# A planned order for linear attention and a two-layer network: first loads, normalisation statistics, one tile's transposition and the planner's model of the DMA queues

## The chip, the cores and the metric

The kernel runs on one core of a Trainium2 chip. The metric is the device time of one execution in microseconds; the median of the runs is used. Three runs of the kernel before gave 218.5, 219.17 and 219.6 us, so the median is 219.17 us.

A core has five engines with a queue of instructions each: PE (matmuls and transposes), DVE and ACT (work on vectors), POOL (work on vectors, and the issuing of DMAs that convert the type on the way) and SP (here only the issuing of DMAs). They run side by side and wait for each other through semaphores. DMA transfers run beside them.

## The reference

Inputs are q, k and v of shape (4 batches, 8 heads, 768 steps, 64), a gain vector of 512 and two weight matrices, 512 x 2048 and 2048 x 512, all fp32. First a recurrence over the steps, with a decay of its own for each head:

```python
gamma = 1.0 - 2.0 ** (-5.0 - np.arange(H, dtype=np.float32))
for t in range(S):
    state = gamma[None, :, None, None] * state + np.einsum('bhd,bhe->bhde', k[:, :, t], v[:, :, t])
    y[:, :, t] = scale * np.einsum('bhd,bhde->bhe', q[:, :, t], state)
```

with scale 1/8. Its result, laid out as (4, 768, 512), is x. Then each row of x is normalised and goes through the two layers:

```python
mu = np.mean(x, axis=-1, keepdims=True)
var = np.mean((x - mu) ** 2, axis=-1, keepdims=True)
xn = (x - mu) / np.sqrt(var + 1e-06) * g_ln
ch = np.maximum(xn @ w_ch1, 0.0) @ w_ch2
return (x + ch).astype(np.float32)
```

## The kernel before

**Tiles.** The 4 x 768 rows are cut into 24 tiles of 128 rows. Tiles 0 to 3 are the first 128 steps of the four batches; then come the five others of batch 0 (tiles 4 to 8), of batch 1 (9 to 13), and so on.

**Attention, per tile.** q and k have to be transposed. For tiles below `T0 = 8` PE does it (lines 395 and 402): ACT copies the transposed k to "trk" (L184) and DVE scales the transposed q into "trq" (L407). From tile 8 on q and k are loaded as a pair into one "qk" buffer, and a DMA on SP's queue transposes the pair into "tr" (L417); DVE then scales the q half into "trq" (L424). PE multiplies the two to the scores "pa" (L434), DVE multiplies them by the decay mask into "asb" (L441), and PE forms y, "py", from asb and v (L457), and from trq and the running state where there is one (L453). For the state, POOL scales v by the decay into "vg" (L510), PE multiplies it with k, "pd" (L522), and DVE turns that into the state in bf16 (L536).

**Normalisation, per tile.** For tiles from 4 on DVE takes the mean and the variance from py with `bn_stats` and `bn_aggr` (L491, L492), then forms xn = (y − mean) · gain (L466), and ACT copies y to "x_all" (L497). For tiles 0 to 3 ACT copies y with a sum on the side (L473), DVE scales the sum to the mean (L479), and ACT squares with another sum, into a "junk" tile, and scales it to the variance (L484, L486). The factor 1/sqrt(var) is applied at the very end: ACT takes the root per group (L572), DVE the reciprocal (L578).

**Layers, per group.** Tiles are grouped for the first layer: six groups of one tile, three of two, three of four. xn is transposed, by PE for tiles below `TX = 8` (L550, copied by ACT to "xnt") and by a DMA on SP's queue from tile 8 on (L564). The first layer (L597) is cut into blocks of 16, 8 or 4 matmuls, which fill one "mm" buffer (there are two); ACT or DVE applies the relu into "h" (L610, L612). The second layer (L634) has four blocks of four matmuls per tile; DVE multiplies by 1/sqrt(var) and adds x (L642), and SP stores the result (L649).

**Loads.** q, k and v tiles (128 KB each in bf16) and the eight weight blocks (512 KB each in bf16) are loaded by POOL's DMAs, which convert from fp32 (L338, L346). Only tile 0 is loaded as fp32 (L324): k and v over SP's queue, q over ACT's, and then cast by ACT and DVE.

**The order.** The order of all instructions is computed before the kernel is built. Every piece of work is a task with an engine (or several to choose from), an estimated duration, a rank, the tasks that it needs, and the buffers that it takes and uses. `Plan.order` simulates the engines with these estimates: it always takes the task that can start first, and among equals the one with the lower rank. What it writes down is the order of the instructions on each engine; times and buffers in the simulation are estimates, and the waits in the built program follow from the data and from the buffers that the tile pools really hand out. In the simulation a task that takes a buffer waits for the buffer of its pool that has been held longest (`oldest = held[name][0]`, lines 68 to 74). Loads share one DMA queue of the model: each occupies it for its estimated time (`dma_free`), and a load may be issued at most `ahead` = 6000 ns before the queue is free. Transpositions by DMA get a fixed latency (`load` 1500, `lat` 5000 for qk; 800 and 4500 for xn), loads from tile 8 on 1500 ns more, and vg from tile 8 on 2500 ns more, so that what uses them is planned later. The first loads of POOL have a fixed rank, in the list `first` (lines 351 to 354). `Plan.fill` puts matmuls on zeros into PE's gaps of the first 20 us (L658).

Of the kernel before, what the change touches and what calls it, by code (L numbers as in the profile page):

```python
# [9 lines left out]
FP32 = mybir.dt.float32  # L10
BF16 = mybir.dt.bfloat16
AF = mybir.ActivationFunctionType
ALU = mybir.AluOpType

PE, ACT, DVE, POOL, SP = range(5)


class Plan:
# [6 lines left out]

    def __init__(self, seen, begin, load_lat, ahead):
        self.seen, self.begin, self.load_lat, self.ahead = seen, begin, load_lat, ahead  # L30
        self.tasks, self.bufs = [], {}
# [4 lines left out]
    def add(self, eng, ns, rank, emit, after=(), takes=None, uses=(), load=0, lat=0, at=0,  # L36
            follows=()):

        t = {"on": eng if isinstance(eng, dict) else {eng: ns}, "rank": rank, "emit": emit,
             "after": list(after), "takes": takes, "uses": list(uses) + ([takes] if takes else []),
             "load": load, "lat": lat, "at": at, "follows": list(follows)}
        self.tasks.append(t)
        return t

    def order(self):
# [8 lines left out]
        dma_free, out = 0, []  # L57
        while any(todo.values()):
            best = None
            for e in engines:  # L60
                for t in todo[e]:
                    if any("end" not in d for d in t["after"] + t["follows"]):
                        continue
                    at = max(free[e], t["at"], dma_free - self.ahead if t["load"] else 0)
                    for d in t["after"]:
                        at = max(at, d["end"] if d["eng"] == e and not d["load"] else d["seen"])
                    at = max([at] + [d["end"] for d in t["follows"]])
                    if t["takes"]:
                        name = t["takes"][0]
                        if len(held[name]) == self.bufs[name]:  # L70
                            oldest = held[name][0]
                            if left[oldest]:
                                continue
                            at = max(at, ends[oldest])
                    if best is None or (at, t["rank"]) < best[0]:
                        best = (at, t["rank"]), t, e
# [8 lines left out]
            if t["load"]:  # L85
                dma_free = max(dma_free, t["end"]) + t["load"]
                t["seen"] = dma_free + self.load_lat + t["lat"]
# [25 lines left out]
def kernel(  # L113
# [21 lines left out]
    P = 128  # L135
# [7 lines left out]
    GROUPS = [1] * 6 + [2] * 3 + [4] * 3  # L143
# [3 lines left out]
    T0, TX = 8, 8  # L147
# [9 lines left out]
                {PE: 900, ACT: 800, DVE: 900, POOL: 1300, SP: 800}, 2250, 6000)  # L157
    ps = bass.MemoryType.PSUM

    def make_pool(name, n, space=None):  # L160
# [7 lines left out]
        for name, n, space in (  # L168
            ("k0", B, None), ("v0", B, None), ("qsb", 6, None), ("ksb", 5, None), ("vsb", 5, None),
            ("qk", 4, None), ("tr", 4, None), ("vg", 3, None), ("trq", 3, None), ("trk", 3, None),  # L170
# [40 lines left out]
    junk = const.tile([P, DM], BF16, name="junk")  # L211
# [77 lines left out]
    def c_gb(eng):  # L289
# [4 lines left out]
        out=grow, in_=moe_g_ln.rearrange("(o n) -> o n", o=1)), load=10)  # L294
# [13 lines left out]
    def load(kind, j, rank):  # L308
        takes, uses, follows = None, [], []
        if kind in "qkv":  # L310
            b, c = TILES[j]
            src = {"q": q, "k": k, "v": v}[kind][b].rearrange("h (c p) d -> c p h d", p=P)[c]
            ns, dma = 910, 780
# [6 lines left out]
            if j == 0:  # L320

                def emit32(eng):
                    dst = take("osb", kind, [P, DM], FP32).rearrange("p (h d) -> p h d", d=D)
                    (nc.scalar if eng == ACT else nc.sync).dma_start(out=dst, in_=src)  # L324
                raw = a(ACT if kind == "q" else SP, 390, -200 + "kqv".index(kind), emit32, (),
                        ("osb", kind), (), 900)

                def emit(eng):
                    evacuate(eng, take(*takes, [P, H, D], BF16),
                             held["osb", kind].rearrange("p (h d) -> p h d", d=D))  # L330
                loaded[kind, j] = a({"k": {ACT: 620}, "q": {DVE: 490}, "v": {ACT: 620, DVE: 430}}[kind], 0, -60, emit,
                                    [raw], takes, [("osb", kind)])
# [6 lines left out]
        else:  # L339
# [3 lines left out]
            ns, dma = 820, 2900  # L343

            def emit(eng):
                nc.gpsimd.dma_start(out=dst, in_=src)  # L346
        loaded[kind, j] = a(POOL, ns, rank, emit, (), takes, uses, dma, 1500 if kind in "qkv" and j > 7 else 0,
                            follows=follows)


    first = ["iota", "pos", "k1", "q1", "v1", "w1_0", "k2", "q2", "v2", "w1_1", "k3", "q3", "v3",
             "w1_2", "k4", "q4", "v4", "w1_3", "k5", "q5", "v5"]
    pool_rank = {x: i - 1000 for i, x in enumerate(first)}
# [7 lines left out]

# [15 lines left out]
    for t in range(NT):  # L377
        g, i = group_of[t]
        rank_of[t] = 10 * t if t < 4 else max(10 * t, 500 + unit["1", g, 0] - 48 + 8 * i)
# [4 lines left out]
    for t in range(NT):  # L384
# [4 lines left out]
        xi = x0 + i4  # L389

# [24 lines left out]
        else:  # L415
            def e_tr(eng, t=t):
# [4 lines left out]
                   1500, 5000)  # L421
# [16 lines left out]
        pat = a(PE, 340, r + 1.2, e_pa, [eq, ek], ("pa", t), [("trq", t), kt])  # L438
# [8 lines left out]
        def e_py(eng, t=t, c=c):  # L447
# [8 lines left out]
            for h in range(H):  # L456
# [6 lines left out]
                ("py", t), [("asb", t), ("trq", t), where["v", t]] + ([("pb", t)] if c else []))  # L463
# [6 lines left out]
        if t < 4:  # L470

            def e_xc(eng, t=t):
                nc.scalar.activation(  # L473
                    out=x_all[:, t, :], in_=held["py", t].rearrange("p h d -> p (h d)"),
                    func=AF.Copy, accum_out=bns[:, t, 0:1])
            xc = a(ACT, 650, r + 2, e_xc, [pyt], uses=[("py", t)])

            def e_me(eng, t=t):
                nc.vector.tensor_scalar_mul(out=mv[:, t, 0:1], in0=bns[:, t, 0:1], scalar1=1.0 / DM)  # L479
            me = a(DVE, 100, r + 2, e_me, [xc])  # L480
            xnn = a(DVE, 750, r + 2, e_xn, [me, gl], ("xn", t), [("py", t)])

            def e_va(eng, t=t):
                nc.scalar.activation(out=junk, in_=x_all[:, t, :], func=AF.Square,  # L484
                                     bias=mv[:, t, 0:1], scale=-1.0, accum_out=bns[:, t, 1:2])
                nc.scalar.activation(out=mv[:, t, 1:2], in_=bns[:, t, 1:2], func=AF.Copy,  # L486
                                     scale=1.0 / DM)
            bn = a(ACT, 900, r + 100, e_va, [me, xc], at=28000 + 2000 * t)
        else:
            def e_bn(eng, t=t):  # L490
                nc.vector.bn_stats(out=bns[:, t, :], in_=held["py", t].rearrange("p h d -> p (h d)"))  # L491
                nc.vector.bn_aggr(out=mv[:, t, :], in_=bns[:, t, :])  # L492
            bn = a(DVE, 880, r + 2, e_bn, [pyt], uses=[("py", t)])
            xnn = a(DVE, 750, r + 3, e_xn, [bn, gl], ("xn", t), [("py", t)])

            def e_xc(eng, t=t):
                nc.scalar.copy(out=x_all[:, t, :].rearrange("p (h d) -> p h d", d=D),  # L497
                               in_=held["py", t])
            xc = a(ACT, 590, r + 2, e_xc, [xnn], uses=[("py", t)])


        if c > 0:
            for cc in ([0, 1] if c == 1 else [c]):
# [4 lines left out]
                def e_vg(eng, j=j, cc=cc):  # L508
# [6 lines left out]
                        lat=2500 if j > 7 else 0)  # L515
# [44 lines left out]
        else:  # L560
            def e_ex(eng, t=t, xb=xb, xi=xi):
                if xi == 0:
# [3 lines left out]
                      [("xn", t)] + ([("xnt", xb)] if xi else []), 800, 4500,  # L566
# [54 lines left out]
    for t, cols in [(t, slice(0, DM)) for t in range(NT - 1)] + [  # L621
# [29 lines left out]
        a(ACT if cols.start else SP, 350, 100, e_st, [add], uses=[("osb", key)])  # L651
# [42 lines left out]
```

## Time and profile before

| What | Value |
|---|---|
| Time, median of 3 runs | 219.17 us (218.5 to 219.6) |
| Span of the profiled execution | 221.8 us |
| PE busy | 209.4 us, 94% of the span |
| DVE, ACT, POOL busy | 118.8, 85.6, 89.3 us |
| First-layer matmuls (L597) | 93.9 us |
| Second-layer matmuls (L634) | 90.4 us |
| Transposition of a qk pair, issue to landing | 6.5 us, median of 16 |
| Transposition of an xn tile, issue to landing | 4.0 us, median of 16 |
| Load of 128 KB by POOL, issue to landing | 6.5 to 8.8 us, medians by kind |
| Load of a weight block, issue to landing | 9.5 us, median of 8 |

The profile is of one execution; the page gives its span and no other time for it. Names such as "tr<-qk" say what an instruction writes and what it reads, "L417" is a line of the kernel. A line of the waits reads: engine, what it was about to do and at which line, what it waited for, the time in total, how often, and the longest. A line of the chain in order of time has the start and the length in us, then what ran. In the slices each digit is a tenth of busy time in a fortieth of the span (5.5 us). "Issue to landing" is the time from a DMA's issue until its semaphore shows it done.

### The profile page before, as it was taken

The numbers are of one execution on the slowest core, as the hardware profiler recorded it, in microseconds if no ns is written. First come the engines' busy times: TensorE is split into PE (matmuls) and PEld (weight loads), VectorE is DVE, ScalarE is ACT, GpSimd is POOL, SyncE is SP. The second block draws the span as 40 slices with busy tenths as digits, with TensorE's granted clock in tenths as the row PEclk, the third lists the DMA queues.
The fourth block names the chain that finished last, engine by engine and source line by source line (L and its number), as shares of the span: only waits on it lengthen the run. The fifth ranks groups of instructions, "written<-read, shape, count | busy, mean of one in ns | idle before, by whom it ended". The sixth has DMA issues, their size and how long they took to land.

```text
span 221.8 us, 4587 instructions
## 1 busy us (share of the span) xinstructions
PE 209.4 (94%) x1896; PEld 131.4 (59%) x1896; DVE 118.8 (54%) x229; ACT 85.6 (39%) x166; POOL 89.3 (40%) x105
## 2 busy tenths in 40 slices
PE   6988999998999999979999958999999999999993
PEld 6677999975756557756676423544444444444453
DVE  6566697974248999959888526562521001111121
ACT  5455688653312113524326241464433343232000
POOL 8996898967065399809059450000000000000000
PEclk9699999999999999999999996999999999999999
DMA  7999999999999999999999999411120011100212
GB/s 145 177 179 181 177 156 204 203 154 109 177 149 158 202 148 136 181 129 187 164 207 110 163 170 126 114 24 24 50 71 14 33 47 50 47 21 26 95 50 95
DMA packets 108326, 26.91 MB, mean 121 GB/s; under 512 B 101009, under 2 KB 105361, under 8 KB 108306
## 3 DMA queue, kind: packets, MB, share of 16 engines
q0 software_dynamic: 75984, 13.24, 82.6%
q1 hardware_dynamic: 31138, 12.98, 31.0%
q10 hardware_dynamic: 1184, 0.39, 0.7%
q8 instruction: 15, 0.25, 0.5%
q14 instruction: 5, 0.04, 0.1%
HBM read 27.27 MB, written 6.29 MB: 151 GB/s over the span
## 4 chain that ended last, share of the span: by engine, by line
PE 75%; DMA 15%; DVE 6%; POOL 1%; issue 1%; POOLq 0%
PE tp L634 34%; PE mm L597 32%; DMA w<-in_moe_w_ch_dram 8%; DMA tr<-qk 7%; PE pa L434 2%; PE py L457 2%; DVE asb L441 2%; PE pd L522 2%; PE py L453 1%; DVE trq L424 1%; DVE osb L642 1%; DVE state L536 1%; DVE bns L491 1%; PE tp L402 0%; PE tp L395 0%
## 5 line engine op out<-in xcount | busy, mean ns | idle before, releaser
L597 PE MATMUL mm<-xnt,w 128*128 128x128 bf16 (+2 forms) x768 | 93.9, 273 | 0.2 <-DMA w<-in_moe_w_ch_dram 0.2
L634 PE MATMUL tp<-w,h 128*128 128x512 bf16 (+1 forms) x400 | 90.4, 375 | 0.6 <-DVE osb L642 0.6
L610 ACT ACTIVATE h<-mm 128x512 bf16<-128x512 f32 x87 | 51.9, 598 | 74.2 <-PE mm L597 74.0
L597 PEld LDWEIGHTS <-w 128*128 128x128 bf16 x768 | 58.3, 98 | 24.3 <-DMA w<-in_moe_w_ch_dram 0.3
L634 PEld LDWEIGHTS <-h 128*128 128x128 bf16 x400 | 38.6, 99 | 41.2 <-issue 2.8
L642 DVE SCALAR_TENSOR_TENSOR osb<-tp,rstd,x_all 128x512 f32<-128x512 f32 (+1 forms) x25 | 18.2, 727 | 63.4 <-PE tp L634 63.2
L441 DVE TENSOR_TENSOR asb<-pa,mask 128x1024 bf16<-128x1024 f32 x24 | 29.3, 1220 | 12.3 <-PE pa L434 12.3
L510 POOL TENSOR_TENSOR vg<-vsb,vsc 128x512 bf16<-128x512 bf16 x16 | 16.9, 1057 | 21.0 <-DMA vsb<-in_v_dram 21.0
L338 POOL DMA_DIRECT2D vsb<-in_v_dram x20 | 18.0, 903 | 4.2 <-PE py L457 2.9
L338 POOL DMA_DIRECT2D qk<-in_k_dram x16 | 14.5, 906 | 12.7 <-DMA tr<-qk 12.6
L497 ACT CAST x_all<-py 128x512 bf16<-128x512 f32 x20 | 11.7, 584 | 19.1 <-DVE xn L466 17.9
L466 DVE SCALAR_TENSOR_TENSOR xn<-py,mv,gb 128x512 bf16<-128x512 f32 x24 | 18.0, 751 | 0.9
L536 DVE TENSOR_TENSOR state<-pd,gch 64x256 bf16<-64x256 f32 x40 | 16.7, 418 | 1.8 <-PE pd L522 1.5
L491 DVE BATCH_NORM_STATS2 bns<-py 128x6 f32<-128x512 f32 x20 | 13.9, 694 | 5.4 <-PE py L457 5.1
L338 POOL DMA_DIRECT2D qk<-in_q_dram x16 | 14.4, 898 | 1.4 <-DMA w<-in_moe_w_ch_dram 1.4
L424 DVE TENSOR_TENSOR trq<-tr,qsc 128x512 bf16<-128x512 bf16 x16 | 7.8, 494 | 9.1 <-DMA tr<-qk 8.9
L457 PE MATMUL py<-vsb,asb 128*128 128x64 bf16 x160 | 8.1, 194 | 3.0 <-DVE asb L441 3.0
L457 PEld LDWEIGHTS <-asb 128*128 128x128 bf16 x192 | 8.1, 100 | 3.2 <-DVE asb L441 3.2
L658 PE MATMUL mm<-zeros 128*128 128x128 bf16 x86 | 8.3, 262 | 1.0 <-DVE zeros L218 1.0
L572 ACT ACTIVATE rstd<-mv,epsb 128x1 f32<-128x1 f32 (+2 forms) x12 | 3.2, 294 | 13.7 <-DVE mv L492 13.7
L453 PEld LDWEIGHTS <-trq 128*128 128x128 bf16 x80 | 6.0, 98 | 3.2
L434 PE MATMUL pa<-trq,tr 64*128 64x128 bf16 x128 | 6.4, 218 | 1.5 <-DVE trq L424 1.5
(68 smaller groups left out, 127.5 us busy)
## 6 DMA issues: line engine op xcount, KB each, us to landing
out_dram<-osb SPq DMA_DIRECT2D x23, 256.0 KB, 2.2
w<-in_moe_w_ch_dram POOLq DMA_DIRECT2D x8, 512.0 KB, 9.5
vsb<-in_v_dram POOLq DMA_DIRECT2D x20, 128.0 KB, 7.8
qk<-in_k_dram POOLq DMA_DIRECT2D x16, 128.0 KB, 6.5
qk<-in_q_dram POOLq DMA_DIRECT2D x16, 128.0 KB, 6.7
qsb<-in_q_dram POOLq DMA_DIRECT2D x7, 128.0 KB, 8.7
ksb<-in_k_dram POOLq DMA_DIRECT2D x4, 128.0 KB, 8.8
k<-in_k_dram POOLq DMA_DIRECT2D x3, 128.0 KB, 7.2
```

The source lines that it names most:

```text
L338: nc.gpsimd.dma_start(out=tile_of(kind, j), in_=src)
L441: nc.vector.tensor_tensor(out=take("asb", t, [P, NPAIR, 2, P], BF16).rearrange("p i a t -> p a i t"), in0=held["pa", t], in1=mask.rearrang ...
L457: nc.tensor.matmul(py[:, h, :], lhsT=held["asb", t][:, h // 2, h % 2, :], rhs=tile_of("v", t)[:, h, :], start=(mi == 0), stop=(mi == n - 1))
L466: nc.vector.scalar_tensor_tensor(out=take("xn", t, [P, DM], BF16), in0=held["py", t].rearrange("p h d -> p (h d)"), scalar=mv[:, t, 0:1], ...
L491: nc.vector.bn_stats(out=bns[:, t, :], in_=held["py", t].rearrange("p h d -> p (h d)"))
L497: nc.scalar.copy(out=x_all[:, t, :].rearrange("p (h d) -> p h d", d=D), in_=held["py", t])
L510: e.tensor_tensor(out=take("vg", j, [P, H, D], BF16), in0=tile_of("v", j), in1=vsc[:, cc, :].unsqueeze(2).to_broadcast([P, H, D]), op=ALU. ...
L536: nc.vector.tensor_tensor(out=held["pb", n][o, :, o], in0=held["pd", b][o, :, o], in1=gch[o, cc, :].unsqueeze(2).to_broadcast([D, NPAIR, D ...
L597: nc.tensor.matmul(p[:, j, :], lhsT=w1[:, ko, (ho + j) * P:(ho + j + 1) * P], rhs=held["xnt", hb][:, h0:h0 + n, ko, :], start=(ko == 0), s ...
L610: nc.scalar.activation(out=dst, in_=src, func=AF.Relu)
L634: nc.tensor.matmul(held[key], lhsT=held["h1", hb][:, ho, i * P:(i + 1) * P], rhs=w2[:, ho, cols], start=(ho == 0), stop=(ho == HO - 1))
L642: nc.vector.scalar_tensor_tensor(out=take("osb", key, [P, w], FP32), in0=held[key], scalar=rstd[:, t:t + 1], in1=x_all[:, t, cols], op0=AL ...
```

## The change

- **Tile 0.** k and v are loaded by POOL with conversion, k before the two `iota` instructions and v after them. q is still loaded as fp32, in two halves, one on SP's queue and one on ACT's, and cast by ACT.
- **First loads.** The list `first` becomes `CFG["first"]`: the first block of w1 comes after the loads of three tiles (before: two), and the list goes on to the last block of w2.
- **bn_stats for all tiles.** Tiles 0 to 3 are treated as the others; the lines with ACT's sums, and the junk tile, go.
- **T0 from 8 to 7.** Tile 7's q and k are loaded as a pair and transposed by DMA.
- **Buffers.** qk 4 to 5, tr 4 to 5, vsb 5 to 6.
- **The planner's model.** Two DMA queues in place of one: `sw_free` for the loads, `hw_free` for transpositions and stores, and each delays the other when both are busy. Waits on another engine from tile 7 on can carry a `slack` of 600 ns. Estimates and pads change: begin of POOL 1300 to 840 and of SP 800 to 740; load 780 to 875, weight block 2900 to 2550, latency of a load 2250 to 700, `ahead` 6000 to 7000; for transpositions `hw` 1600 and a pad of 2500, 830 and 1500 for xn; vg pad 2500 to 1000, load pad 1500 to 500 (from tile 7 on); pa 340 to 410; store 350 to 400 with `hw` 450.

In the built program this gives, beside the new first loads, these orders. On POOL the loads of k and q of tile 12 stand ahead of the vg of tile 9 (before: behind the vg of tile 12), and k of tile 12 is given the qk buffer of tile 8. On PE the matmuls pd of tile 9 stand right behind the transposes of tile 7's xn, and the first layer of tiles 8 and 9 after two blocks of tile 6's second layer (before: three). On DVE the trq of tiles 20 and 21 both stand ahead of tile 19's statistics (before: that of tile 20).

```diff
+CFG = {
+    "T0": 7, "TX": 8, "groups": [1] * 6 + [2] * 3 + [4] * 3,
+    "first": ["k0", "iota", "pos", "v0", "k1", "q1", "v1", "k2", "q2", "v2", "w1_0",
+              "k3", "q3", "v3", "w1_1", "w1_2", "k4", "q4", "v4", "k5", "q5", "v5", "w1_3",
+              "w2_0", "k6", "q6", "v6", "k7", "q7", "v7", "w2_1", "w2_2", "w2_3"],
+    "bufs": {"qsb": 6, "ksb": 5, "vsb": 6, "qk": 5, "tr": 5, "vg": 3, "trq": 3, "trk": 3},
+    "load_pad": 500, "lead": 48, "step": 8,
+    "slack": 600, "tr_pad": 2500, "x_pad": 1500, "vg_pad": 1000,
+}
...
-                    at = max(free[e], t["at"], dma_free - self.ahead if t["load"] else 0)
+                    at = max(free[e], t["at"], sw_free - 7000 if t["load"] else 0)
                     for d in t["after"]:
-                        at = max(at, d["end"] if d["eng"] == e and not d["load"] else d["seen"])
+                        if d["eng"] == e and not d["load"] and not d["hw"]:
+                            at = max(at, d["end"])
+                        else:
+                            at = max(at, d["seen"] + t["slack"])
...
             if t["load"]:
-                dma_free = max(dma_free, t["end"]) + t["load"]
-                t["seen"] = dma_free + self.load_lat + t["lat"]
+                sw_free = max(t["end"] + 800, sw_free) + t["load"]
+                t["seen"] = sw_free + 700 + t["lat"]
+            if t["hw"]:
+                begun = max(at + 600, hw_free)
+                queued = max(0, sw_free - begun)
+                hw_free = begun + t["hw"] + min(queued, 2 * t["hw"])
+                if queued:
+                    sw_free += t["hw"] * 2 // 3
+                t["end"] = free[e] = max(t["end"], hw_free - 900)
+                t["seen"] = hw_free + 1050 + t["lat"]
...
-    T0, TX = 8, 8
+    T0, TX = CFG["T0"], CFG["TX"]
...
-                {PE: 900, ACT: 800, DVE: 900, POOL: 1300, SP: 800}, 2250, 6000)
+                {PE: 900, ACT: 800, DVE: 900, POOL: 840, SP: 740}, 3600)
...
-            if j == 0:
...
-                raw = a(ACT if kind == "q" else SP, 390, -200 + "kqv".index(kind), emit32, (),
-                        ("osb", kind), (), 900)
+            if j == 0 and kind == "q":
+                raws = []
+                for half, eng in ((0, SP), (1, ACT)):
+                    hs = slice(half * H // 2, (half + 1) * H // 2)
...
+                        (nc.scalar if eng == ACT else nc.sync).dma_start(out=dst, in_=src[:, hs])
...
-        loaded[kind, j] = a(POOL, ns, rank, emit, (), takes, uses, dma, 1500 if kind in "qkv" and j > 7 else 0,
-                            follows=follows)
-
-
-    first = ["iota", "pos", "k1", "q1", "v1", "w1_0", "k2", "q2", "v2", "w1_1", "k3", "q3", "v3",
-             "w1_2", "k4", "q4", "v4", "w1_3", "k5", "q5", "v5"]
-    pool_rank = {x: i - 1000 for i, x in enumerate(first)}
+        loaded[kind, j] = a(POOL, ns, rank, emit, (), takes, uses, dma,
+                            lat=LOAD_PAD if kind in "qkv" and j >= T0 else 0, follows=follows)
+
+    pool_rank = {x: i - 1000 for i, x in enumerate(FIRST)}
...
             ek = a(SP, 1230, r - 16, e_tr, [loaded["k", t], loaded["q", t]], ("tr", t), [("qk", t)],
-                   1500, 5000)
+                   hw=1600, lat=TR_PAD)
...
-        pat = a(PE, 340, r + 1.2, e_pa, [eq, ek], ("pa", t), [("trq", t), kt])
+        pat = a(PE, 410, r + 1.2, e_pa, [eq, ek], ("pa", t), [("trq", t), kt], slack=slack)
...
-        if t < 4:
-
-            def e_xc(eng, t=t):
-                nc.scalar.activation(
-                    out=x_all[:, t, :], in_=held["py", t].rearrange("p h d -> p (h d)"),
-                    func=AF.Copy, accum_out=bns[:, t, 0:1])
...
+        def e_bn(eng, t=t):
+            nc.vector.bn_stats(out=bns[:, t, :], in_=held["py", t].rearrange("p h d -> p (h d)"))
+            nc.vector.bn_aggr(out=mv[:, t, :], in_=bns[:, t, :])
+        bn = a(DVE, 880, r + 2, e_bn, [pyt], uses=[("py", t)])
...
-                        lat=2500 if j > 7 else 0)
+                        lat=VG_PAD if j > 7 else 0)
...
             ex[t] = a(SP, 1200, r + 4, e_ex, [xnn], ("xnt", xb) if xi == 0 else None,
-                      [("xn", t)] + ([("xnt", xb)] if xi else []), 800, 4500,
+                      [("xn", t)] + ([("xnt", xb)] if xi else []), hw=830, lat=X_PAD,
                       follows=[ex[t - 1]] if xi else [])
...
-        a(ACT if cols.start else SP, 350, 100, e_st, [add], uses=[("osb", key)])
+        a(ACT if cols.start else SP, 400, 100, e_st, [add], uses=[("osb", key)], hw=450)
```

## The prediction, made before the changed kernel had run

> **What bounds the kernel now.** I read the totals and the slices first, then where the chain of work spends its time, the waits, and the stretches.
>
> ```profile
> span 221.8 us, 4587 instructions
> ...
> PE 209.4 (94%) x1896; PEld 131.4 (59%) x1896; DVE 118.8 (54%) x229; ACT 85.6 (39%) x166; POOL 89.3 (40%) x105
> ...
> PE   6988999998999999979999958999999999999993
> ...
> DMA  7999999999999999999999999411120011100212
> ...
> PE 75%; DMA 15%; DVE 6%; POOL 1%; issue 1%; POOLq 0%
> ```
>
> PE is busy 94%, and the DMA engines are full for 25 slices of 5.5 us, to about 139 us. So only PE's idle time and its extra work can pay; everything else matters by making PE wait. By stretches (columns: us, PE, PEld, DVE, ACT and POOL busy, granted clock):
>
> ```profile
> 0.00:22.50 22.50, 18.70 (x261) 15.95 (x262) 14.09 (x44) 11.57 (x26) 19.05 (x29) 0.92 1.61 170
> 22.50:47.30 24.80, 24.77 (x459) 23.75 (x456) 20.44 (x40) 19.02 (x43) 20.44 (x24) 1.00 1.82 182
> 47.30:85.00 37.70, 37.08 (x308) 22.37 (x306) 24.67 (x44) 9.78 (x18) 21.74 (x24) 1.00 1.79 157
> 85.00:140.00 55.00, 50.47 (x448) 31.56 (x446) 39.62 (x73) 19.51 (x35) 28.10 (x31) 0.97 1.70 158
> ```
>
> From 22.5 to 85 us PE loses 0.65 us, so nothing is to be won there, only lost. Idle time lies at the start (3.8 us, beside warm-up matmuls that count as busy) and in 85–140 (4.5 us). The waits say whose:
>
> ```profile
> POOL qk L338 <- DMA tr<-qk: 12.6, 2, 8.7
> DVE trq L424 <- DMA tr<-qk: 8.9, 4, 4.4
> ...
> PE py L457 <- DVE asb L441: 3.0, 1, 3.0
> PE pa L434 <- DVE trq L424: 1.5, 2, 1.2
> ```
>
> The 3.0 is this piece of the chain in order of time:
>
> ```profile
> 126.30 5.81 DMA tr<-qk
> 132.11 0.02 issue
> 132.13 0.43 DVE trq L424
> 132.56 1.15 DVE asb L441
> 133.70 0.04 issue
> 133.75 0.54 PE py L457 x8
> 134.28 5.00 PE tp L634 x16
> ```
>
> A late transposition stops PE, and the restart costs more: 16 second-layer matmuls take 5.00 us, against 3.33 before the stop; the clock granted in 134.3–140 was 0.74. So the late stretch loses 3.0 + 1.6 here and 1.2 at 98.5 us: 5.8. One POOL line and the transpositions' latencies carry the rest:
>
> ```profile
> 113.61 0.89 POOL L338 DMA_DIRECT2D qk<-in_k_dram  x1 [8.67 <-DMA tr<-qk]
> ```
>
> ```profile
> tr<-qk SPq DMA_TRANSPOSE x16, 6.5
> xnt<-xn SPq DMA_TRANSPOSE x16, 4.0
> ```
>
> Singly, tiles 8 to 10 took 9.3, 9.9 and 10.0 us from issue to landing, tile 11 5.7, the late ones 4.9 to 9.6, the last (few loads left) 3.2.
>
> **What the skill says.** The Trainium skill, "DMA: Bandwidth & Descriptors", section "Issuing engines are not separate DMA queues": DMAs of all issuers run on the same 16 engines and interleave. The trace agrees: a transposition takes 9.3 us among loads, 3.2 alone. Same page, "Queues, rings and completion order": each DMA engine goes round its queue rows by packets, so a transposition is shared with the loads, not put behind them. Same page, "Anatomy of one DMA — SWDGE (gpsimd) path": a semaphore wait happens on the issuing sequencer. That is the 8.67 us above: POOL stood, with its multiplications and later loads behind it.
>
> **Part by part.** The span is taken as the profiled execution's time (the page gives no other); it stands 2.6 over the median of 219.17. I add differences in us to the median.
>
> *Start.* k0 and v0 are loaded first on POOL's queue, and w1's first block comes after three tiles' loads instead of two. Before, k of tile 1 was issued at 1.37 and landed at 7.56 (6.2); the next tiles came 0.86 apart, w blocks 2.0–3.3, say 2.6. After: k0 lands at 4.5–7.0, I take 5.3; q0 goes over SP and ACT, so eight loads (k0 v0, k1 q1 v1, k2 q2 v2) stand ahead of w1_0: 5.3 + 7×0.86 + 2.6 = 13.9 (13.1–15.6). Before, the first w1 matmul ran at 14.89. Gain 1.0.
>
> *Tile 7 by DMA:* 8 PE transposes less (2×0.22 = 0.44) and one ACT copy less (0.59, on an engine with room); one more DMA transposition, 17 for 16 (3.2 alone), on the queue that is late. Start and this: −1.4 (−2.2 to +0.5).
>
> *bn_stats for tiles 0–3:* DVE gains 694 + 182 − 152 = 724 ns a tile, 2.9 in all; ACT loses 597 + 199 + 729 + 196 + 203 − 584 = 1340 ns a tile, 5.4. DVE was busy 14.1 of 22.5, so 8.4 us of idle time covers it; from py to xn tile 0 takes 0.69 + 0.18 instead of 0.60 + 0.20 + 0.15 and waits. Taken as nothing (−0.5 to +0.7; uncovered, +2.9).
>
> *POOL's order and the qk slots (5 for 4).* The planner takes the oldest-held slot as free. In the build, tile 12's k takes tile 8's slot, so it waits for tile 8's transposition to land; behind it in POOL's queue come q12 and vg9 (before: vg9 to vg12 stood ahead of k12). vg9 is wanted by pd9, which stands in PE's order right behind tile 7's transposes. PE gets there so: first w2 block before at 47.32, less 1.4 and rounding, 45.8; 11 blocks of four w2 matmuls 9.5, pa, py and tx of tile 7 1.0: 56.3. vg9 is ready at: tile 8's transposition issued at 47.7 as before (two more tiles lie on the load queue by then, +1.7, which starts up to 2.3 earlier), landing 8.7 later (5.7–9.9), k12 0.9, q12 0.9, vg9 1.06: 59.3. PE stops 3.0 (0–4.2), and I add 0.5 for a lower clock at the restart (0–1.6): **+3.5**.
>
> *Group 7's first layer* stands after two blocks of tile 6's second layer (before three) and needs tile 9's x transposition. PE reaches it 23.8 us of work after pd9 (15 w2 blocks 13.0, 8 w1 blocks 6.9, five pa, four py, two pd 3.9): 83.1. Before, that transposition landed at 78.68 for use at 84.20, 5.5 to spare. Now py9 follows pd9's stop, its xn is ready at 74.9, and on SP it stands behind tile 12's transposition, a store and tile 13's: landing 80–85. Stop 0–4, taken as **+1.2**.
>
> *Late.* bn_stats of tile 19 now stands on DVE behind trq of tiles 20 and 21 (before: of 20 alone); ACT's square root of group 10 waits for it, relus of group 9 stand behind that, and with two "mm" buffers PE stops 2.6 us later. k21 now waits as k20 did (113.6); two loads and SP's queue bring its transposition to 118.7–121.5, landing 5.8 (to 9.9) later: 124.5–131.4, +1.6 for trq, bn_stats and root. PE, shifted by some 2.8, gets through py19 at 125.7 and can go to 128.3. Stop 0–4.7, say 2.4, clock 1.6; the waits for transpositions before it 1.5, after it 1.3: 6.8 for the old 5.8: **+1.0** (−5 to +3).
>
> More buffers for tr and vsb and the costs themselves act only through these orders.
>
> Sum: −1.4 + 0 + 3.5 + 1.2 + 1.0 = **+4.3: 223.5 us**.
>
> **Rivals.**
> (a) *Faster, 213–216.* Earlier loads and pads win most of the late 5.8, and tile 8's transposition lands within 5.7 us of its issue as tile 11's did, so that pd9 doesn't wait: 219.2 − 1.4 − 2 to −5. For: five slots, loads earlier. Against: tiles 8–10 took 9.3–10.0 while loads flowed. It decides at 5.7.
> (b) *About the same, 218.1–221.* pd9's stop is half of mine (1.5) and paid by the start (1.4); the late waits are as before. For: the queue starts earlier. Against: bn of tile 19 has a new wait.
> (c) *The transpositions' queue becomes the bound, 226.5–230.* Loads and 33 transpositions fill the same engines to 139 us; each late group waits 1–2 more, at five places: +4.3 + 3 to 6. For: DMA at 9. Against: about the same bytes, one transposition more.
> (d) *The change doesn't do what it says:* the planner's slot model isn't the build's. That is in my main case; if the model held, k12 would not wait, and it would be (a).
>
> **How the numbers follow.** No difference that can be told is within 0.5%, 1.1 us (218.07–220.27). Chances: main case (221–226.5) 0.55; (a) 0.12; (b) 0.20, of it 0.08 within the bound and 0.12 above; (c) 0.13. Slower: 0.55 + 0.12 + 0.13 = 0.80. The range leaves out (a) and the end of (c): 218.2–228.5; the main case's own is 221–226.5.
>
> **What would show it.** Right: first w1 matmul near 14; POOL idle some 5 us near 50–57 for a qk load that waits for a tile's transposition; PE idle 3 at pd near 56; a stop at the first-layer matmuls near 83 waiting for xnt; PE idle at 125–133 behind relu and the square root. Wrong: no idle POOL there, vg9 done by 56, PE's idle time in 85–140 under 4 us; or tile 8's transposition issued well before 47.7.

## The result and the profile after

The changed kernel takes 230.34 us (median of 4 runs, 229.44 to 232.47), the kernel before 219.38 us over the runs made beside it. The ratio is 1.051, with a 95% interval of 1.045 to 1.057: 11 us slower, where I had forecast 4.3 (223.5 us) and a range up to 228.5. Ratios leave out executions that took over 1.5% more than the fastest of the same kernel and medians don't, so the two can differ, most of all for b_t7, where 11 of 17 are left out.

The totals, the slices and the shares of the chain, of the profile after:

```profile
span 230.6 us, 4560 instructions
...
PE 213.8 (93%) x1888; PEld 132.6 (57%) x1888; DVE 118.4 (51%) x229; ACT 81.2 (35%) x151; POOL 91.3 (40%) x107
...
PE   8969999999459999999999968999999999999994
...
PEclk9999999999959999999999995999999999999999
...
PE 69%; DMA 21%; POOL 6%; issue 1%; DVE 1%; ACT 0%; POOLq 0%
```

PE has two holes, in the slices from 58 to 69 and from 133 to 144 us, and in the second slice of each it was granted about half its clock. DMA has grown in the chain from 15 to 21%, POOL from 1 to 6%. By the same stretches as before (us, then PE, PEld, DVE, ACT and POOL busy, granted clock, DMA share, GB/s):

```profile
0.00:22.50 22.50, 19.08 (x233) 15.44 (x234) 14.13 (x42) 10.21 (x22) 19.31 (x29) 1.00 1.51 146
22.50:47.30 24.80, 24.30 (x452) 23.61 (x450) 19.91 (x41) 15.82 (x32) 20.08 (x24) 1.00 1.79 181
47.30:85.00 37.70, 31.30 (x250) 18.87 (x247) 15.98 (x29) 8.62 (x16) 21.11 (x24) 0.91 2.24 145
85.00:140.00 55.00, 51.91 (x488) 32.84 (x487) 43.97 (x81) 18.67 (x35) 30.79 (x33) 0.98 1.79 170
```

Most of the loss is in the third stretch: PE idle 6.4 us (before 0.6), at a mean clock of 0.91. The waits (engine, work and line, what it waited for; us in all, times, longest):

```profile
POOL qk L358 <- DMA tr<-qk: 12.1, 3, 6.7
...
PE pd L520 <- POOL vg L508: 6.1, 2, 5.6
...
PE mm L595 <- ACT h L608: 3.1, 1, 3.1
PE mm L595 <- DMA w<-in_moe_w_ch_dram: 2.0, 2, 1.7
```

And the chain in order of time around the three stops (start, length, what ran):

```profile
8.84 7.81 DMA w<-in_moe_w_ch_dram
...
53.37 8.73 DMA tr<-qk
...
62.98 0.43 POOL qk L358
...
63.84 0.17 POOL qk L358
...
64.73 1.07 POOL vg L508
...
65.85 0.58 PE pd L520 x4
66.43 1.71 PE tp L632 x4
68.14 2.70 PE mm L595 x16
...
126.45 10.64 DMA tr<-qk
137.09 0.02 issue
137.11 0.43 DVE trq L441
137.54 0.62 DVE bns L489
138.18 0.19 DVE mv L490
138.40 0.30 ACT rstd L570
138.70 0.49 ACT h L608
139.19 0.04 issue
139.23 1.87 PE mm L595 x4
```

The middle block is the forecast chain, link by link: tile 8's transposition lands at 62.10, only then POOL issues k and q of tile 12, only then it computes vg of tile 9, and pd starts at 65.85. The last block is the other forecast chain: trq of tile 21, then tile 19's statistics, the root, the relu, and only then PE. The places were right; the sizes of the first two were not.

Line by line of my sum, by when the same piece of work starts on PE in the two profiles: the first second-layer matmul at 47.32 before and 48.60 after (+1.3); the 65th, past the first hole, at 72.47 and 80.92 (+8.4); PE's last at 218.42 and 227.24 (+8.8). So the two spans differ by 8.8. The medians differ by 11, because the one profiled execution of the kernel before was slower than usual; the second profile of it (below) spans 218.1. A time is some 1.9 us longer than the span of the same execution (232.47 and 230.6 here, 219.94 and 218.1 there). By my estimate the first profiled execution of the kernel before, of span 221.8, thus took some 223.7 us, 4.5 over the median; I had compared the span itself with the median and seen only 2.6.

### The profile page after: what moved, and what is told of

Same layout as the page of the kernel before. It is cut to its first block, busy times and chain, and to the rows that moved or that the text cites. A ratio compares the mean times of both kernels' runs of the same rounds, so it can differ in the third digit from the quotient of the medians.

```text
span 230.6 us, 4560 instructions
## 1 busy us (share of the span) xinstructions
PE 213.8 (93%) x1888; PEld 132.6 (57%) x1888; DVE 118.4 (51%) x229; ACT 81.2 (35%) x151; POOL 91.3 (40%) x107
## 4 chain that ended last, share of the span: by engine, by line
PE 69%; DMA 21%; POOL 6%; issue 1%; DVE 1%; ACT 0%; POOLq 0%
PE tp L632 31%; PE mm L595 30%; DMA tr<-qk 8%; DMA vsb<-in_v_dram 5%; DMA qk<-in_q_dram 5%; DMA w<-in_moe_w_ch_dram 3%; PE pa L451 2%; PE py L470 2%; PE pd L520 2%; POOL vg L508 2%; PE py L474 2%; POOL k L358 1%; POOL v L358 1%; POOL qsb L358 1%; POOL qk L358 1%
## 5 line engine op out<-in xcount | busy, mean ns | idle before, releaser
L595 PE MATMUL mm<-xnt,w 128*128 128x128 bf16 (+2 forms) x768 | 96.1, 277 | 5.1 <-ACT h L608 3.1
L608 ACT ACTIVATE h<-mm 128x512 bf16<-128x512 f32 x89 | 53.1, 598 | 77.2 <-PE mm L595 77.1
L489 DVE BATCH_NORM_STATS2 bns<-py 128x6 f32<-128x512 f32 x24 | 16.7, 696 | 18.7 <-PE py L474 18.7
L495 ACT CAST x_all<-py 128x512 bf16<-128x512 f32 x24 | 14.0, 584 | 22.4 <-DVE xn L484 21.7
L508 POOL TENSOR_TENSOR vg<-vsb,vsc 128x512 bf16<-128x512 bf16 x16 | 17.0, 1063 | 10.6 <-DMA vsb<-in_v_dram 7.5
L358 POOL DMA_DIRECT2D qk<-in_k_dram x17 | 15.6, 918 | 12.1 <-DMA tr<-qk 12.1
L520 PE MATMUL pd<-vg,qk 128*128 128x128 bf16 x52 | 5.5, 233 | 5.6 <-POOL vg L508 5.6
L656 PE MATMUL mm<-zeros 128*128 128x128 bf16 x86 | 9.6, 269 | 1.0 <-DVE zeros L232 1.0
L520 PEld LDWEIGHTS <-qk 128*128 128x128 bf16 x52 | 4.0, 104 | 7.5 <-issue 6.2
L656 PEld LDWEIGHTS <-zeros 128*128 128x128 bf16 x86 | 7.6, 126 | 1.1 <-DVE zeros L232 1.0
```

What stands on the lines that cost most here:

```text
L358: nc.gpsimd.dma_start(out=tile_of(kind, j), in_=src)
L508: e.tensor_tensor(out=take("vg", j, [P, H, D], BF16), in0=tile_of("v", j), in1=vsc[:, cc, :].unsqueeze(2).to_broadcast([P, H, D]), op=ALU. ...
L520: nc.tensor.matmul(held["pd", b][:, i, :], lhsT=tile_of("k", j)[:, 2 * i:2 * i + 2, :], rhs=held["vg", j][:, 2 * i:2 * i + 2, :], start=(c ...
L595: nc.tensor.matmul(p[:, j, :], lhsT=w1[:, ko, (ho + j) * P:(ho + j + 1) * P], rhs=held["xnt", hb][:, h0:h0 + n, ko, :], start=(ko == 0), s ...
L608: nc.scalar.activation(out=dst, in_=src, func=AF.Relu)
L656: nc.tensor.matmul(held["mm", "warm"][:, 0:P], lhsT=zeros, rhs=zeros, start=True, stop=True)
```

## Experiments

| Kernel | Median us | Ratio to before (95%) |
|---|---|---|
| after | 230.34 | 1.051 (1.045–1.057) |
| a_fifo: buffers in turn | 228.64 | 1.042 (1.034–1.050) |
| a_vg9: loads behind vg | 228.37 | 1.034 (1.027–1.041) |
| a_t8: tile 7 on PE | 229.76 | none |
| a_fifo_first2: w1 earlier | 229.09 | 1.026 (1.017–1.035) |
| a_pads: old pads | 223.69 | 1.018 (1.011–1.024) |
| a_fifo_pads | 222.60 | 1.011 (1.005–1.017) |
| a_fp_t8: and tile 7 on PE | 220.85 | 1.000 (0.997–1.003) |
| a_fp_start: and the old start | 218.98 | 0.995 (0.993–0.998) |
| a_fp_t8_start: and both | 217.56 | 0.989 (0.986–0.992) |
| z_gb | 218.55 | 0.993 (0.990–0.995) |
| b_again: before, once more | 219.94 | – |
| b_fifo: before, buffers in turn | 219.60 | 0.996 (0.994–0.999) |
| b_start: before, new start | 220.94 | 1.003 (1.000–1.006) |
| b_t7: before, tile 7 by DMA | 222.44 | 1.003 (0.998–1.008) |
| b_bn: before, bn_stats for all | 217.68 | 0.989 (0.986–0.992) |
| b_fifo_bn | 218.64 | 0.996 (0.993–0.998) |

### The stop at pd of tile 9: a_fifo, a_vg9

a_fifo gives the qk pairs their five buffers in turn, which is what the planner assumed; the order stays:

```diff
-        held[pool, key] = pools[pool].tile(shape, dtype, name=pool, tag=pool)
+        if pool == "qk":
+            i = (key - T0) % 5
+            held[pool, key] = qk_slot[i].tile(shape, dtype, name=f"qk{i}", tag=f"qk{i}")
+        else:
+            held[pool, key] = pools[pool].tile(shape, dtype, name=pool, tag=pool)
```

> The changed kernel with its order untouched; only the qk pairs take their five buffers in turn (tile t takes number (t-7) mod 5), so k of tile 12 takes tile 7's buffer and not tile 8's. Theory A (the stop at pd of tile 9 is POOL standing at k of tile 12, and nothing else holds PE there): POOL doesn't wait there, vg of tile 9 is done by about 59, the stop of 5.55 and its slow restart of 2.2 go: 222 to 224; since k of tile 21 no longer waits for tile 18's transposition either, the stop near 139 shrinks or goes too: down to 219. Rival B (the DMA engines are full there and set the pace): PE stops for something else between 56 and 90, at trq of tile 8 or the x transposition of tile 9: 227 to 230.

a_vg9 leaves the buffers and moves two loads:

```diff
+        pick = [t for t in planned if t is loaded["k", 12] or t is loaded["q", 12]]
+        planned = [t for t in planned if t not in pick]
+        n = planned.index(vg_of[9]) + 1
+        planned[n:n] = pick
```

> The changed kernel with only one move: on POOL the loads of k and q of tile 12 go behind vg of tile 9 instead of ahead of it; the buffers are as they were, so k of tile 12 still waits for tile 8's transposition. Theory A: only what stands behind the wait matters, so the stop at pd of tile 9 goes and the later stop near 139 stays: 222.5 to 225.5. Rival B (full DMA engines): 227 or more.

Both take the stop away: neither profile has PE idle at a pd in 50 to 70 us. But the medians fall by some 2 us (by the ratios 0.8% and 1.6%, and a_fifo's interval overlaps that of the changed kernel), not by 7.7. The times are in Rival B's ranges, and Theory A's "nothing else holds PE there" falls. PE's waits in a_vg9:

```profile
PE mm L596 <- ACT h L609: 5.7, 1, 5.7
PE mm L596 <- DMA xnt<-xn: 2.3, 1, 2.3
PE mm L596 <- DMA w<-in_moe_w_ch_dram: 2.3, 1, 2.3
```

The stop behind the square root grew from 3.1 to 5.7, and the wait of group 7's first layer for tile 9's x transposition, which I had put at 1.2 and which the changed kernel didn't show, is there with 2.3 (1.3 in a_fifo; a_fifo's stop behind the root is 2.7). The long stop at pd had covered both. A stop that is removed uncovers the next ones; the rest of the loss had to be looked for elsewhere.

### What the pads are worth: a_pads, a_fifo_pads

```diff
-    "load_pad": 500, "lead": 48, "step": 8,
-    "slack": 600, "tr_pad": 2500, "x_pad": 1500, "vg_pad": 1000,
+    "load_pad": 1500, "lead": 48, "step": 8,
+    "slack": 600, "tr_pad": 5000, "x_pad": 4500, "vg_pad": 2500,
```

> As a_fifo, with the four pads of the kernel before (transposition 5000, xn 4500, vg 2500, loads 1500), so that the order is planned anew with what uses a transposition standing later. Theory C (the small pads put the attention of the late tiles too early in PE's and DVE's order, with too little layer work ahead of it): the stop behind the square root near 135 (2.7 and its slow restart) and the waits of 1.3, 0.7, 0.8 and 0.9 between 85 and 132 go in large part: 222 to 225. Rival B (the DMA engines are full whatever the order): 227 to 230.

> The changed kernel with the four old pads, and the qk buffers as the build hands them out (as a_fifo_pads without the buffers in turn; the order is the same). On POOL k of tile 12 again stands ahead of vg of tile 9 and waits for tile 8's transposition. Theory A: a stop of 3 to 5.5 at pd of tile 9 and its slow restart: 225 to 228. Rival: with the old pads pd of tile 9 stands later on PE too and the wait is covered: 222 to 223.5.

a_fifo_pads has the buffers in turn as well. The pads are the largest single piece: 1.051 to 1.018 with the four pads alone, 1.042 to 1.011 with the buffers in turn. Theory C's time came true (222.60 us), and Rival B's 227 to 230 did not. In the late stretch of a_pads PE doesn't stop at all:

```profile
47.30:85.00 37.70, 34.77 (x287) 20.93 (x285) 16.53 (x31) 9.71 (x18) 21.33 (x24) 0.95 2.13 162
85.00:140.00 55.00, 55.00 (x518) 34.66 (x517) 48.42 (x88) 21.02 (x38) 30.65 (x33) 1.00 1.71 165
```

Against the changed kernel PE is busy 3.1 us more in 85–140 (there 51.91), and 3.5 more in 47.30–85 (there 31.30), where the stop at pd is shorter. This pair alone doesn't tell whether the order or the transfers changed: the DMA share and GB/s are nearly the same (1.71 and 165, 1.79 and 170), but the transpositions of tiles 19 to 22 took 4.4, 6.7, 6.1 and 4.7 us from issue to landing, in the changed kernel 7.4, 8.5, 10.6 and 6.2. The pair a_fifo and a_fifo_pads, one profile each, tells more. With the small pads they took 9.6, 9.8, 8.9 and 8.1, and with the old pads 9.5, 9.3, 9.7 and 8.3, no shorter in all, and yet PE's late stops go (first a_fifo, then a_fifo_pads):

```profile
100.00:150.00 50.00, 45.16 (x372) 25.97 (x373) 34.39 (x61) 17.24 (x32) 20.26 (x22) 0.97 1.31 140
100.00:150.00 50.00, 49.68 (x443) 29.81 (x445) 39.35 (x74) 23.45 (x42) 19.50 (x21) 1.00 1.58 140
```

So in the late stretch the small pads had asked for the results too early, and the old order covers transpositions that are just as slow. It does not cover every one: in a_fifo_pads group 7's first layer waits 4.3 us, before 93.03, for tile 9's x transposition, which took 8.9. In a_pads tile 19's statistics run at 132.60, ahead of the trq of tiles 20 and 21 (134.22 and 135.53); in the changed kernel they stood behind both (137.46, behind 132.94 and 137.11). a_fifo_pads has the order of a_pads (131.71, 133.33 and 136.85). The stop at pd of tile 9 is still in a_pads, 2.9 us before 66.14, just under the 3 to 5.5 of Theory A: it was right on that wait and wrong on the time (225 to 228; the rival's 222 to 223.5 was just missed too). The step from a_pads to a_fifo_pads is 0.7%, and their intervals overlap; that the buffers in turn help there is likely, not shown.

One thing works against them. In each of four pairs of profiles that differ by the buffers in turn, the transpositions of qk pairs take longer where POOL no longer stands before a load: medians of 6.7 and 8.6 us (changed kernel, a_fifo), 5.8 and 8.5 (a_pads, a_fifo_pads), 6.6 and 7.9 (b_again, b_fifo), 6.9 and 7.0 (b_bn, b_fifo_bn). That this is why the buffers in turn gain so little is likely, not shown.

### Start and tile 7

b_start and b_t7 each put one part on the kernel before: the tile-0 loads and the head of the list `first` as in the change's diff, and

```diff
-    T0, TX = 8, 8
+    T0, TX = 7, 8
```

> The kernel before with the new start alone: tile 0's k and v by POOL, q in two halves, and w1's first block behind three tiles' loads (the old planner plans the rest anew). Theory D (the start costs, because w1's first block then lands near 16.6 instead of 11.2, and eight loads on POOL's queue instead of six stand ahead of tile 8's): 220.5 to 222.5. Rival (the start gains, as I predicted): 218 to 219.5.

> The kernel before with T0 at 7 alone (the old planner plans anew). Theory E (one more transposition among the loads takes 2.5 us of the load queue, so that tile 8's and all later ones are late): 221 to 223.5. Rival (it takes the place of PE's and ACT's work and is hidden): 218.7 to 220.

Alone each costs 0.3% by the ratios, with intervals from one up to 1.006 for b_start and on both sides of one for b_t7. The medians, 220.94 and 222.44 (before: 220.25 beside them), lie in the ranges of Theories D and E. b_t7's times scatter: over all 17 its median is 1.0% above that of before. What the two parts do to the load queue is plain in the traces, though. Tile 8's q, whose landing lets its transposition start, landed at 47.64 in the kernel before, at 50.27 in b_start, at 50.07 in b_t7, and at 53.35 in the changed kernel: 2.6 and 2.4 alone, 5.7 together. In b_start w1's first block lands at 18.03 (before: 11.17), and PE starts on it at 18.08 (before: 14.89); the profile ends only 0.6 later than that of b_again (218.7, 218.1), so that most of this is made up later. The chain in order of time:

```profile
8.78 9.25 DMA w<-in_moe_w_ch_dram
18.04 0.05 issue
18.08 1.07 PE mm L603 x16
```

and in b_t7, whose profiled execution took 223.28 us, and where vg of tile 9 comes behind the loads of tile 11 (k of tile 11 waits for tile 8's transposition there):

```profile
38.91 11.15 DMA qk<-in_q_dram
...
50.13 7.99 DMA tr<-qk
...
58.66 0.84 POOL qk L338
...
60.42 1.07 POOL vg L510
...
61.53 0.58 PE pd L522 x4
```

During tile 7's transposition (issued 34.73, landed 47.99 in b_t7) the weight blocks landed 3.1, 3.4 and 4.1 us apart; in the kernel before 2.5 to 2.6. That is where the 2.4 us come from. In the changed kernel the blocks that land during tile 7's transposition (39.06 to 51.7) do so at 43.29, 46.43 and 49.83, 3.1 and 3.4 us apart. The profile of b_t7 also has a stop of 4.1 us at pd of tile 9; it is one execution, and that the stop is usual isn't shown.

On the changed kernel's side the same two were taken back one by one, from a_fifo_pads:

> a_fifo_pads with T0 at 8 and the new start kept. The new start and tile 7's transposition each put 2.5 us on the load queue ahead of tile 8; if each costs its half of the 5 us that both cost: 219.5 to 220.7. If the transposition is nearly all of it: 217.5 to 219. If the start is: 221.3 to 223.

> a_fifo_pads with the old start and T0 kept at 7. Halves: 219.5 to 220.7. If the start was nearly all: 217.5 to 219. If the transposition of tile 7 was: 221.3 to 223.

> a_fifo_pads with the start of the kernel before (tile 0 over SP and ACT, w1's first block behind two tiles) and with T0 at 8, so that of the change there remain bn_stats, the buffers and the planner's two queues with the old pads. If start and tile 7 are what is left of the loss: 217 to 219.5. Rival (the planner's queues or the buffers cost by themselves): 220.5 to 223.

The edits are

```diff
-    "T0": 7, "TX": 8,
+    "T0": 8, "TX": 8,
```

for tile 7, and for the start tile 0's three fp32 loads as in the kernel before, and

```diff
-    "first": ["k0", "iota", "pos", "v0", "k1", "q1", "v1", "k2", "q2", "v2", "w1_0",
-              "k3", "q3", "v3", "w1_1", "w1_2", "k4", "q4", "v4", "k5", "q5", "v5", "w1_3",
+    "first": ["iota", "pos", "k1", "q1", "v1", "w1_0", "k2", "q2", "v2", "w1_1",
+              "k3", "q3", "v3", "w1_2", "k4", "q4", "v4", "w1_3", "k5", "q5", "v5",
```

By the ratios tile 7 is worth 1.1% (1.011 to 1.000), the start 1.6% (1.011 to 0.995), both together 2.2%: 2.4, 3.5 and 4.8 us of 219, nearly a sum. The start is the larger of the two by the expectations too: a_fp_start (218.98) lies in the range for "the start was nearly all", a_fp_t8 (220.85) just above the one for equal halves; the intervals of the two ratios touch, though. What is left of the change, bn_stats, the buffers and the planner's two queues, with the old pads and the buffers in turn, is 1.1% faster than before. That is what bn_stats alone gives (b_bn below), so no effect of the rest can be told. In the profile of a_fp_t8_start PE is busy 54.58 of the 55 us from 85 to 140, where the kernel before's two profiles had 50.47 and 52.08.

An earlier try at the start and one at tile 7, both while the small pads were in, told less:

> As a_fifo, with the first block of w1 behind two tiles' loads instead of three (after v1). The first w1 matmul comes near 14 instead of 16.5. Theory D (the start costs what w1's first block is late): 225.5 to 227. Rival: tiles 2 and 3 are then late by as much, and the first layer has to wait for them: 227.5 to 229.

> The changed kernel with T0 at 8: tile 7 is transposed by PE again, and the order is planned anew from there. Theory A with its second part (the transposition of tile 7 takes 2.5 us from the load queue and so delays the loads and the transposition of tile 8): that transposition is issued near 50.8 instead of 53.4, the stop at pd of tile 9 is 2.5 to 3.5 instead of 5.55: 225 to 227.5. Rival (the transposition of tile 7 is free, the loads are late for another reason): issued at 53 as now, 229.5 to 231.

The edit of a_t8 is the one for tile 7 above; that of a_fifo_first2, on top of a_fifo, is

```diff
-              "k1", "q1", "v1", "k2", "q2", "v2", "w1_0",
+              "k1", "q1", "v1", "w1_0", "k2", "q2", "v2",
```

a_fifo_first2 had runs from 225.2 to 231.7, and its profile shows another late stop, 4.7 us at a py waiting for ACT; against a_fifo the intervals overlap. a_t8 (T0 at 8) ran from 225.9 to 230.7; tile 8's transposition was issued at 49.5 rather than 53.4 (the second part of Theory A: 50.8), and no stop at pd of tile 9 is left (Theory A: 2.5 to 3.5). But a first-layer matmul then waited 6.8 us for an x transposition before 127.80 in the one execution that was profiled, and no gain can be told. All four profiles of repairs with the small pads have a late stop of 2.7 to 6.8 us.

### The kernel before again, and its parts: b_again, b_fifo, b_bn, b_fifo_bn

> The kernel before once more, unchanged, for a second profile. If the late stop of PE in the first profile (3.0 us before 133.75, with its slow restart) is not usual, the span is 217.5 to 219.5 and PE is idle for less than 1.5 us between 120 and 140; if it is usual, the span is 221 to 222 and the stop is there again.

Span 218.1. PE's waits:

```profile
PE mm L597 <- ACT h L610: 1.4, 1, 1.4
PE pa L434 <- DVE trq L424: 1.2, 1, 1.2
```

The stop of 3.0 us with the slow restart isn't there; 1.4 us near it, at a first-layer matmul before 129.51, is. So the late 5.8 us, on which my sum rested, were mostly of that one execution: between 85 and 140 PE is idle 2.9 us here, at full clock.

> The kernel before with its order untouched; only the qk pairs take their four buffers in turn. Theory A (POOL's wait of 8.67 us at 113.6 is what makes the transpositions of tiles 20 and 21 late): that wait goes or shrinks below 4 us, the stop of PE at 131 to 134 and its slow restart (3.0 and 1.6) go: 214.5 to 217. Rival B: the loads come earlier but so do their collisions with the transpositions, which land as late as before: 218.5 to 220.5.

The edit is a_fifo's with four buffers on the kernel before. 0.4% faster, in Rival B's range of times: POOL's wait for a transposition is gone from its profile, as Theory A wanted, but what that was to win, the late stop, was not there in the second profile of the kernel before either. PE's longest late wait in b_fifo is 0.9 us.

b_bn drops the branch for tiles 0 to 3 and nothing else:

```diff
-        if t < 4:
...
-        else:
-            def e_bn(eng, t=t):
+        def e_bn(eng, t=t):
```

> The kernel before with bn_stats for tiles 0 to 3 too, and nothing else; the order is planned anew. As predicted, DVE's 2.9 us more lie in its idle time: 218.5 to 220.5. Rival 1: the shorter way from py to xn lets the first layer start 0.8 to 1.2 earlier and that is kept: 217.5 to 218.5. Rival 2: DVE makes tiles 2 and 3 late: 221 or more.

1.1% faster, 217.68 us. That is the first rival's time, but not by its mechanism: PE's 129th first-layer matmul starts at 27.50 us in b_again and at 27.46 in b_bn, and the fifth addition of a second-layer result on DVE at 76.16 and 76.17, while the last one starts 3.1 us earlier (214.71, 211.61). So in these profiles the gain arises late, not at the start: the order planned anew has no stop above 0.3 us after 25 us, where b_again has stops of 1.2 and 1.4.

> The kernel before with bn_stats for all tiles and with the qk buffers in turn. If what the two gave alone (1.1% and 0.4%) adds: 216.3 to 217.4. Rival (the statistics alone already took the stops away): 217.4 to 218.5.

b_bn with b_fifo's edit: 218.64 rather than 217.68, just outside both expected ranges. The two don't add, and with buffers in turn b_bn is slower. Its profile has waits of 1.3, 0.4 and 0.5 us for trq and the state between 85 and 119 that b_bn's hasn't. POOL's wait of 6.5 us for a transposition, which b_bn has, is gone; taking it away is not a gain by itself.

> a_fp_t8_start with the latency of the gain vector's load set to 6000 ns in the plan, so that PE doesn't wait 2.4 us for it near 6.7 ahead of the first tile. If those 2.4 us carry through the start: 215 to 216.7. Rival (the start is set by w1's first block or by tile 0's path on DVE anyway, and the order later gets worse): 217.2 to 219.

The edit, on a_fp_t8_start, is at the gain vector's load:

```diff
-        out=grow, in_=moe_g_ln.rearrange("(o n) -> o n", o=1)), lat=2500)
+        out=grow, in_=moe_g_ln.rearrange("(o n) -> o n", o=1)), lat=6000)
```

The wait of 2.4 us is gone and the time is not shorter than a_fp_t8_start's (the ratio is 0.4 points higher, and the intervals overlap). The rival's range holds; which of its reasons is the cause isn't shown.

a_fp_t8_start and b_bn, both 0.989 (0.986–0.992), are the fastest: 1.1% below the kernel before, and so below the changed one by more.

## Why the prediction was wrong

Two steps failed most. The sum let tile 8's loads come as early as before, although a later start and one more transposition stood ahead of them, which made the stop at pd too small. And it gave the smaller pads no term. The bullets go by place in the profile; the experiments go by edit: old pads take 3.3% away, the buffers in turn 0.7, the old start and tile 7 together 2.2 (1.051, 1.018, 1.011, 0.989). The two accounts cut the same loss in two ways and don't add.

- **Direction and mechanisms: right.** Slower was given 0.80, and both PE stops that I named, at pd and behind the square root, are there, with the waits, lines and orders that I named. With the old pads the change is still 1.8% slower, so the direction doesn't hang on what I left out. That a_pads, at 223.69 us, is so near my 223.5 is in part luck: its stop at pd is 2.9, 3.0 in my sum, but the start loses where I had a gain, and the late stretch loses nothing.
- **Start and tile 7, −1.4: measured +1.3 in the profile.** The step "5.3 + 7×0.86 + 2.6" failed: w1's first block was issued at 8.84 instead of 4.13, and landed 7.81 later (before 7.04): 16.66, not 13.9. The eight landings from k0 on were 5.16, 6.75, 8.00, 8.95, 9.77, 10.62, 11.43 and 13.70. The first and four of the distances are as I took them. The others are not: 1.59 and 1.25 after k0 (v0 was issued 1.50 after k0, with the two `iota` instructions between them), 2.27 before the last, and 2.96 from there to w1's block. Why the last load takes so long is open.
- **Tile 8's transposition "issued at 47.7 as before": measured 53.37.** This is the costliest error in the profile. I took the two more tiles (+1.7) as paid by a queue that starts earlier; b_start shows +2.6. And I priced tile 7's transposition at 3.2 on its own queue and at nothing for the loads, although I had quoted the Trainium skill, "DMA: Bandwidth & Descriptors", section "Issuing engines are not separate DMA queues", that all DMAs run on the same engines; b_t7 shows that it holds the loads back by 2.4, which agrees with the page. With landing after 8.7, as assumed, vg of tile 9 was ready at 65.8 (59.3 in my sum). PE came later as well, at 60.3 instead of 56.3, so the stop was 5.55 for 3.0.
- **The restart, +0.5: measured 2.2.** pd, four second-layer and sixteen first-layer matmuls took 0.58, 1.71 and 2.70 us; at full clock 0.22, 0.86 and 1.75. With the last two the line of my sum for pd, +3.5, measured +7.1.
- **Group 7's first layer, +1.2: no stop.** It was masked by the longer stop before it and came out once that was removed: 1.3 in a_fifo, 2.3 in a_vg9, 4.3 in a_fifo_pads.
- **bn_stats at nothing: wrong on the other side.** Alone it is worth −1.1%, and in the profiles this comes late, with the order planned anew, and not at the start.
- **Late, +1.0 against the old 5.8: measured +0.4 in the profiles.** The mechanism was right, the 5.8 was not the kernel's but one execution's. Against b_again the changed kernel loses some 3.7 more; that is why the medians part by 11 and the spans by 8.8, the profiled execution after being itself 2 over its median.
- **Rival (c)**, the transpositions' queue as the bound, came closest to the time (226.5 to 230) for the wrong reason. The transpositions did become slower (xn: median 4.0 and 5.0 in the two profiles before, 6.3 after), but a_fifo_pads covers late ones of 8.3 to 9.7 us with 0.3 us of idle time on PE from 100 to 150, so they are not the bound there. What cost most, 3.3%, was an edit that I had put in one clause, "the costs themselves act only through these orders". It is true, and I had followed two of these orders only.
- **Rival (d)**, that the planner's buffers aren't the build's, is true, and worth about 2 of the 11 us by a_fifo, not clear of noise.

Open: which of the four pads matters, since they were only put back together; and what the new order of b_bn owes to the statistics themselves, since any edit makes the planner order anew.

## What to carry to other kernels

When an order is planned from estimates, a pad on a transfer's latency buys cover: cut it, and consumers move ahead of the work that hid the wait; late qk transpositions of 8 to 10 us stopped PE with the small pads (a_fifo) and not with the old ones (a_fifo_pads). A transfer that takes work off an engine is paid on the queue that it shares; look for who waits for the next landing there. And before resting a sum on a stall of one profiled execution, compare that execution's time, not its span, with the spread of the times: here it was some 4 us off.

## What the runs showed of the hardware

- One DMA transposition of a qk pair among loads took 12.6 us from issue to landing in the changed kernel and 13.3 in b_t7, and pushed the loads behind it back by about 2.4 us in b_t7; alone, late in the run, one took 3.2.
- After an idle of 5.55 us and after one of 3.09 PE ran at half speed (four second-layer matmuls in 1.71 us for 0.86): the granted clock of the changed kernel was 0.50 from 63.13 to 69.96 and from 138.22 to 145.05, both times 6.83 us. This cost 2.2 and 3.0 us. An idle of 2.72 us in a_fifo was followed by a clock of 0.50 from 136.0 to 139.4; after 2.30 us in a_vg9 (86.9 to 93.0) and 1.36 in b_again it stayed at 1.00. The Trainium skill, "TensorE: Matmul & The Clock Gate", section "Part 1: The HAM clock gate (the "warmup" mystery)", tells of this: the array's clock is halved after at least one idle window of about 3.4 us and restored after a busy one. The traces agree on the factor of two; here 2.7 to 3.1 us of idle time were enough.
- Two profiles of the same kernel, before, differ by 3.7 us in span, nearly all of it in the late transpositions and what follows them: the tenth addition of a second-layer result on DVE starts at 113.42 and 113.04, the twelfth at 139.32 and 135.57.
